# Block transforms of a state-space layer: float32 matrix products in place of three products of half-precision parts

## The chip, the cores and the metric

The kernel runs on one core of a Trainium2 chip. The metric is the device time of one execution in microseconds (us). A profiled execution beside it gives each engine's instructions: TensorE (PE, its weight loads PEld), VectorE (DVE), ScalarE (ACT), GpSimd (POOL) and the queues that issue transfers, above all SyncE's (SP).

## The reference

A sequence x of 2048 rows and 512 channels passes two layers. Each adds a long convolution of its normalised rows, and then a gated feed-forward product of the normalised result:

```
x = x + ssm(layernorm(x)); x = x + ffn(layernorm(x))     # twice, same weights
ssm(u): K[d, l] = Re(sum_n C[d, n] exp(dt A[d, n] l) dt B[d, n]);  y = causal_conv(u, K) + u * Dskip
ffn(x): (silu(x @ w_gate) * (x @ w_up)) @ w_down          # 512 -> 1376 -> 512
```

The reference makes the convolution by FFTs of length 4096. All is float32.

## The kernel before

**Blocks.** The sequence is cut into four blocks of 512 rows. The convolution works on block spectra: the block is normalised, transformed forward (`forward`, line 257), multiplied channel by channel with the filter's spectra, summed over the block and the earlier ones, and transformed back (`inverse`, line 770). Block b of a layer needs b + 1 products of spectra, so blocks 0 to 3 cost VectorE very different amounts. Eight (layer, block) pairs are worked in the order `SEQ` = (0,0), (0,1), (0,2), (1,0), (0,3), (1,1), (1,2), (1,3).

**Stages.** About the first 300 us make the filter's spectra and the split weights from the parameters; their order on the engines is written out by hand (`plan`, `at`). From then on the eight feed-forward blocks run, each as two halves of 256 rows (`ffn`, line 918). The loop at the end issues the convolution of pair i + 1 ahead of the feed-forward of pair i, and a scheduler that ranks instructions by given priorities sets the order on each engine when the program is built; the order is then fixed and each engine works its list from the front.

**A half of the feed-forward.** TensorE makes ten times 24 products of 128x256 half-precision tiles (lines 930, 931 and 933: the weights and the activations are each split in a high and a low half-precision part, three products for one), 48 small ones for the 96 columns that are left over (897 to 899), and 66 products 512 wide for the second matrix (945 to 947). VectorE multiplies gate and up (937), makes the low part (939) and adds the result to the block (950, twice per half). PSUM for these comes from one pool of two large buffers (`pbig`).

**The convolution.** One pass over a half of the channels (`ssm_half`, line 746) does four spectra. For each, line 810 multiplies two 128x1024 tiles and line 813 adds them up (first spectrum: 810 alone), 818 and 819 join the complex parts, 765 and 766 are butterflies; 831 to 843 prepare four tiles for `inverse`, and `result` (line 786) adds the result to the block. The first two pairs take their forward spectra by `direct` or `second`, and their inverse transform by float32 products.

**What the change touches.** From pair (0,2) on, both transforms use the way of the feed-forward. In `forward`, line 265 (ACT) and line 266 (through the helper `stt`, whose instructions carry line 230 on DVE) split the normalised tile n in two half-precision parts z; line 275 issues three products per pair of tiles; 276 to 278 scale and combine. In `inverse`, line 774 (ACT) and 775 (`stt`, line 230) split each tile v in parts yl, scaled by `sy`, and line 782 issues six products where the float32 branch issues two. The scale `sy` is made at run time: `sizes` (line 614) sums the magnitudes of the taps on ACT, once for each of eight chunks of channels, `direct_size` adds the skip term, and `product_scale` turns it into powers of two. The generator `inputs` (line 710) yields forward spectra, and `ssm_half` takes the next one from it at each of its four steps, so that one spectrum is ready ahead.

Of the kernel before, what the change touches and what calls it, by code (L numbers as in the profile page):

```python
# [22 lines left out]
P = 128  # L23
# [16 lines left out]
HALF = 2  # L40
INV = 2
# [4 lines left out]
def dft_constants():  # L46
# [21 lines left out]
    halves = []  # L68
    for e in (er * 256.0, ei * 8192.0):
        hi = e.astype(np.float16)  # L70
        halves.append(np.stack([hi, (e - hi).astype(np.float16)], 3))
    return [a.astype(np.float32) for a in (ef, ei, ek)] + [am] + halves
# [3 lines left out]
def kernel(ctx, tc, x, a_re, a_im, b_re, b_im, c_re, c_im, log_dt, d_skip,  # L76
                           w_gate, w_up, w_down, c_ef, c_ei, c_ek, c_am, c_eh, c_eih, out):
# [53 lines left out]
    wsum = sb.tile([P, NCH], F32, name="wsum")  # L131
    sy = sb.tile([P, 4], F32, name="sy")
    wmax = sb.tile([P, 2], BF16, name="wmax")
# [55 lines left out]
    dmax = sb.tile([1, 1], F32, name="dmax")  # L189

    def direct_size():

        da = tl([1, D], "da", "sg")
        A.activation(da, dsk, AF.Abs)
        V.tensor_reduce(dmax, da, axis=AX.X, op=OP.max)

# [60 lines left out]
    def forward(n, h, eh):  # L257


        if not fss:  # L260
            ft = tl([P, 3, 2, HD], "fbt", "bt")
            fss.extend([ft[:, i] for i in range(3)] + [tl([P, 2, HD], "fu", "u") for _ in range(3)])
            fs.extend(fss)
        hs = slice(h * HD, (h + 1) * HD)
        A.activation(z2[:, 0], n[:, :, hs], AF.Copy, scale=256.0)
        stt(z2[:, 1], n[:, :, hs], 256.0, z2[:, 0], OP.subtract)
        sums = []
        for pair in ((0, 2), (1, 3)):
            d_, s_ = fs.pop(0), fs.pop(0)
            pf = [psml([P, 2, HD], "pf") for _ in pair]  # L270
            with tc.high_priority(offset=BOOST):
                for r, p in zip(pair, pf):
                    for i in range(2):
                        for k, (le, lz) in enumerate(((0, 0), (0, 1), (1, 0))):
                            PE.matmul(p[:, i], lhsT=eh[:, r, i, le], rhs=z2[:, lz, r], start=k == 0, stop=k == 2)
                A.activation(d_, pf[0], AF.Copy, scale=2.0 ** -16)
            stt(s_, pf[1], 2.0 ** -16, d_, OP.add)
            stt(d_, pf[1], -2.0 ** -16, d_, OP.add)
# [333 lines left out]
    def sizes(ch, kt, junk):  # L612

        A.activation(junk, kt, AF.Abs, accum_out=wsum[:, ch:ch + 1])

    def product_scale():

        V.tensor_reduce(sy[:, 0:1], wsum, axis=AX.X, op=OP.max)  # L620
        V.tensor_tensor(sy[0:1, 0:1], sy[0:1, 0:1], dmax, OP.add)
# [680 lines left out]
```

## Time and profile before

| what | value |
|---|---|
| median of 3 runs | 1112.01 us (1109.95 to 1116.78) |
| the profiled execution | 1118.76 us, of which the span of its instructions is 1117.0 us |
| granted TensorE clock over the span | 0.982 |
| matrix products recorded | 9302 |
| bytes moved by transfers | 149.23 MB |

The profile lists for each engine the time in which it was busy. A matrix product's record is longer than the distance to the next one (they are pipelined), and DVE's records overlap a little in the same way, so the price of one in a full queue is the distance between two starts. In a row of groups stands the source line, the engine, the tile written and those read, the shape, the count, the busy time, the mean of one in ns, and the idle time of the engine just before them with what ended it. In a row of the time line stand the start, the length, the engine and line, and in brackets the idle time before it with its releaser. A row of stages gives for a stretch of the span each engine's busy time, the granted clock (1.00 is full speed) and the share of the transfer engines.

### The profile page before, as it was taken

To read this page: it belongs to the slowest core of one execution; us is meant where nothing else is said; L and a number is where in the kernel's file an instruction comes from. 1 tells how busy PE (TensorE), PEld (TensorE's weight loads), DVE (VectorE), ACT (ScalarE), POOL (GpSimd) and SP (SyncE) were. 2 spreads that over 40 slices of the span, in tenths; PEclk is the share of its full clock that TensorE was granted. 3 is DMA by queue.
4 is the path that set the end of the run, shared out by engine and by line. 5 is a ranking of instruction groups with operands and counts; after the bars stand their busy time and mean duration, and the time that the engine had idled before them with its cause. 6 is when DMAs were issued, how large, how long until landed. Compare 5 with 4: busy or idle time off the path is not lost.

```text
span 1117.0 us, 22795 instructions
## 1 busy us (share of the span) xinstructions
PE 1034.6 (93%) x9302; PEld 812.1 (73%) x9302; DVE 969.8 (87%) x1405; ACT 548.9 (49%) x1093; POOL 105.1 (9%) x163
## 2 busy tenths in 40 slices
PE   2989999998788999899999999989999999999998
PEld 1868888887676768686858677767768686786774
DVE  8999999999999998999999989999994899972221
ACT  6989999942483245464553154524315532143210
POOL 0112222220000010110000011100000000000000
PEclk9989999998999999999999999999999999999999
DMA  5367777767765455422453562354343244302000
GB/s 207 123 174 174 170 169 178 186 182 269 234 214 96 147 158 188 152 76 54 146 141 100 144 210 86 109 167 112 132 138 109 67 138 147 123 20 56 2 25 20
DMA packets 125003, 149.23 MB, mean 134 GB/s; under 512 B 50897, under 2 KB 75985, under 8 KB 124130
## 3 DMA queue, kind: packets, MB, share of 16 engines
q1 hardware_dynamic: 112994, 122.27, 36.1%
q0 software_dynamic: 11904, 25.50, 9.8%
q8 instruction: 73, 1.20, 0.5%
q14 instruction: 32, 0.26, 0.1%
HBM read 97.66 MB, written 33.82 MB: 118 GB/s over the span
## 4 chain that ended last, share of the span: by engine, by line
DVE 43%; PE 32%; issue 11%; DMA 7%; ACT 4%; POOL 2%; SPq 1%; DVEq 0%; POOLq 0%; ACTq 0%
PE pgu L930 5%; PE pgu L933 4%; PE pgu L931 4%; PE pw L542 4%; DVE t L810 4%; DVE yk L813 3%; DVE yk L810 3%; DMA mix<-nn 3%; DVE g L483 3%; PE py L945 3%; PE py L946 2%; PE py L947 2%; DMA n<-xdr 2%; DVE sg L937 2%; DVE g L497 2%
## 5 line engine op out<-in xcount | busy, mean ns | idle before, releaser
L930 PE MATMUL pgu<-mix,wsl 128*128 128x256 f16 x1280 | 300.4, 274 | 11.9 <-DVE sg L937 5.3
L931 PE MATMUL pgu<-mix,wsl 128*128 128x256 f16 x1280 | 300.2, 274 | 0.0
L933 PE MATMUL pgu<-mix,wsl 128*128 128x256 f16 x1280 | 196.2, 274 | 0.0
L945 PE MATMUL py<-wsl,hh 128*128 128x512 f16 (+1 forms) x352 | 136.0, 386 | 17.8 <-DVE xg L950 15.0
L931 PEld LDWEIGHTS <-wsl 128*128 128x128 f16 x1280 | 125.7, 98 | 31.1 <-issue 14.3
L930 PEld LDWEIGHTS <-wsl 128*128 128x128 f16 x1280 | 125.7, 98 | 18.5 <-issue 1.2
L947 PE MATMUL py<-wsl,hl 128*128 128x512 f16 (+1 forms) x352 | 135.7, 385 | 1.9 <-DVE hl L939 1.8
L933 PEld LDWEIGHTS <-wsl 128*128 128x128 f16 x1280 | 125.8, 98 | 15.5
L946 PE MATMUL py<-wsl,hh 128*128 128x512 f16 x320 | 123.8, 387 | 0.0
L936 ACT ACTIVATE sg<-pgu,sc 128x512 f32<-128x512 f32 x80 | 54.5, 681 | 137.0 <-PE pgu L933 136.9
L813 DVE TENSOR_TENSOR yk<-yk,t 128x1024 f32<-128x1024 f32 x96 | 116.7, 1215 | 0.4
L810 DVE TENSOR_TENSOR t<-uu,w 128x1024 f32<-128x1024 f32 x96 | 116.6, 1215 | 0.1
L937 DVE SCALAR_TENSOR_TENSOR sg<-pgu,sc,sg 128x512 f32<-128x512 f32 x80 | 59.5, 744 | 54.6 <-ACT sg L936 54.5
L938 ACT ACTIVATE hh<-sg 128x512 f16<-128x512 f32 x80 | 50.2, 627 | 86.9 <-DVE sg L937 86.9
L542 PE MATMUL pw<-kt,ek 128*128 128x256 f32 (+1 forms) x384 | 90.8, 373 | 0.0
L542 PEld LDWEIGHTS pw<-kt,ek 128*128 128x128 f32 x384 | 72.3, 193 | 8.5
L946 PEld LDWEIGHTS <-hh 128*128 128x128 f16 (+1 forms) x352 | 34.9, 99 | 56.8 <-issue 21.7
L507 PE MATMUL pk<-re,g 128*32 128x64 f32 x1024 | 65.1, 317 | 2.7 <-DMA g<-g 1.6
L939 DVE TENSOR_TENSOR hl<-sg,hh 128x512 f16<-128x512 f32 x80 | 54.7, 684 | 14.4 <-ACT hh L938 14.4
L947 PEld LDWEIGHTS <-hl 128*128 128x128 f16 (+1 forms) x352 | 34.9, 99 | 43.4 <-issue 3.0
L508 PE MATMUL pk<-im,g 128*32 128x64 f32 x1024 | 63.2, 301 | 0.0
L945 PEld LDWEIGHTS <-hh 128*128 128x128 f16 (+1 forms) x352 | 34.9, 99 | 35.6 <-issue 2.9
(265 smaller groups left out, 2007.1 us busy)
## 6 DMA issues: line engine op xcount, KB each, us to landing
uu<-udr SPq DMA_DIRECT2D x96, 256.0 KB, 3.0
w<-wdr SPq DMA_DIRECT2D x96, 256.0 KB, 2.7
g<-g POOLq DMA_DIRECT2D x6, 1024.0 KB, 9.1
udr<-fu POOLq DMA_DIRECT2D x22, 256.0 KB, 2.9
udr<-u SPq DMA_DIRECT2D x16, 256.0 KB, 3.4
n<-xdr SPq DMA_DIRECT2D x4, 1024.0 KB, 7.1
kdr<-ks SPq DMA_DIRECT2D x6, 512.0 KB, 3.1
kt<-kdr SPq DMA_DIRECT2D x24, 128.0 KB, 3.0
```

What stands on the lines that cost most here:

```text
L507: PE.matmul(o, lhsT=g[:, 0, :, d], rhs=re[:, 0:64, d], start=True, stop=False, tile_position=(0, 32 * grp))
L508: PE.matmul(o, lhsT=g[:, 1, :, d], rhs=im[:, 0:64, d], start=False, stop=True, tile_position=(0, 32 * grp))
L542: PE.matmul(pw[:, i], lhsT=e, rhs=kt[:, :, c + 4 * k0:4 * k1:4, :].rearrange("p g k d -> p k g d"), start=c == 0, stop=c == 3)
L810: V.tensor_tensor(t, uu.unsqueeze(2).to_broadcast([P, NQ, 2, 2, DC]), w.unsqueeze(3).to_broadcast([P, NQ, 2, 2, DC]), OP.mult)
L813: V.tensor_tensor(yk, yk, t, OP.add)
L930: PE.matmul(o, lhsT=wgu(wi, k, 0)[:, fs], rhs=nh[:, k], start=k == 0, stop=False)
L931: PE.matmul(o, lhsT=wgu(wi, k, 1)[:, fs], rhs=nh[:, k], start=False, stop=False)
L933: PE.matmul(o, lhsT=wgu(wi, k, 0)[:, fs], rhs=nlo[:, k], start=False, stop=k == 3)
L937: V.scalar_tensor_tensor(sg, pgu[:, 1], sc6[:, 4:5], sg, OP.mult, OP.mult)
L945: PE.matmul(py[:, r], lhsT=hh[:n, f, rc], rhs=wd(f, 0)[:n], start=f == 0, stop=False)
L946: PE.matmul(py[:, r], lhsT=hh[:n, f, rc], rhs=wd(f, 1)[:n], start=False, stop=False)
L947: PE.matmul(py[:, r], lhsT=hl[:n, f, rc], rhs=wd(f, 0)[:n], start=False, stop=f == FT - 1)
```

## The change

The half-precision parts of both block transforms go. `forward` multiplies n by float32 constants in one product per pair of tiles; `inverse` has only its float32 branch; the adds behind them lose their scale factors. `sizes`, `direct_size`, `product_scale` and the tiles z, yl, `sy` and `eih` go with them, and the two halved constant tables (512 KB each) give way to one float32 table `er` of 512 KB. Two buffers for forward spectra are added (`fz`, in the room of z), and from the third pair on `ssm_half` holds two spectra ahead instead of one.

```diff
-    def forward(n, h, eh):
+    def forward(n, h):
         if not fss:
-            ft = tl([P, 3, 2, HD], "fbt", "bt")
-            fss.extend([ft[:, i] for i in range(3)] + [tl([P, 2, HD], "fu", "u") for _ in range(3)])
+            ft, fz = tl([P, 3, 2, HD], "fbt", "bt"), tl([P, 2, 2, HD], "fz", "z")
+            fss.extend([ft[:, i] for i in range(3)] + [fz[:, i] for i in range(2)])
+            fss.extend(tl([P, 2, HD], "fu", "u") for _ in range(3))
             fs.extend(fss)
         hs = slice(h * HD, (h + 1) * HD)
-        A.activation(z2[:, 0], n[:, :, hs], AF.Copy, scale=256.0)
-        stt(z2[:, 1], n[:, :, hs], 256.0, z2[:, 0], OP.subtract)
...
                     for i in range(2):
-                        for k, (le, lz) in enumerate(((0, 0), (0, 1), (1, 0))):
-                            PE.matmul(p[:, i], lhsT=eh[:, r, i, le], rhs=z2[:, lz, r], start=k == 0, stop=k == 2)
-                A.activation(d_, pf[0], AF.Copy, scale=2.0 ** -16)
-            stt(s_, pf[1], 2.0 ** -16, d_, OP.add)
-            stt(d_, pf[1], -2.0 ** -16, d_, OP.add)
+                        PE.matmul(p[:, i], lhsT=er[0][:, r, i], rhs=n[:, r, hs], start=True, stop=True)
+                A.activation(d_, pf[0], AF.Copy)
+            V.tensor_tensor(s_, d_, pf[1], OP.add)
+            V.tensor_tensor(d_, d_, pf[1], OP.subtract)
...
-    def sizes(ch, kt, junk):
-        A.activation(junk, kt, AF.Abs, accum_out=wsum[:, ch:ch + 1])
...
         def inverse(pi, r, v):
-            if half:
-                yl = yl2[0][:, r % 2]
-                A.activation(yl[:, 0], v, AF.Copy, scale=sy[:, 0:1])
-                stt(yl[:, 1], v, sy[:, 0:1], yl[:, 0], OP.subtract)
             with tc.high_priority(offset=0 if first else BOOST):
-                if half:
-                    terms = [(eih[:, r, i, le], yl[:, ly, i]) for i in range(2) for le, ly in ((0, 0), (0, 1), (1, 0))]
-                else:
-                    terms = [(ei[:, r, i], v[:, i]) for i in range(2)]
-                for k, (e, o) in enumerate(terms):
-                    PE.matmul(pi[:, r % 2], lhsT=e, rhs=o, start=k == 0, stop=k == len(terms) - 1)
+                for i in range(2):
+                    PE.matmul(pi[:, r % 2], lhsT=ei[:, r, i], rhs=v[:, i], start=i == 0, stop=i == 1)
             done(v)
...
-            if half:
-                stt(o, pi, sy[:, 1:2], o, OP.add)
-            else:
-                V.tensor_tensor(o, o, pi, OP.add)
+            V.tensor_tensor(o, o, pi, OP.add)
...
+        depth = 1 if SEQ.index((layer, b)) < 2 else 2
...
-            nxt = next(spec, None)
-            if nxt:
+            while len(ahead) < depth and (nxt := next(spec, None)):
                 ahead.append(nxt)
```

Since the scheduler ranks anew, the lists of all engines change from about the first feed-forward products on. Two places on VectorE matter below.

The first is the inverse transform of pair (0,2), near the end of the first feed-forward block's second half. In the rows, line 831 to 843 prepare the tiles (`bb`, `mix`), `yl` is the low half-precision part, `yk` and `t` are the sums and products of spectra of the pair. Before:

```order
L831 TENSOR_TENSOR bb<-bb,mix 128x512
L950 SCALAR_TENSOR_TENSOR xg<-py,sc_92,xg 128x512
L813 TENSOR_TENSOR yk<-yk,t 128x1024
L834 TENSOR_TENSOR mix<-bb 128x256
L835 TENSOR_TENSOR mix<-bb 128x256
L839 TENSOR_TENSOR bb<-bb,mix 128x512
L230 SCALAR_TENSOR_TENSOR yl_4065<-bb,sy,yl_4065 128x512
L810 TENSOR_TENSOR t<-uu,w 128x1024
L842 TENSOR_TENSOR bb<-bb 128x256
L843 TENSOR_TENSOR bb<-bb 128x256
L230 SCALAR_TENSOR_TENSOR yl_4065<-mix,sy,yl_4065 128x512
```

Now, where the changed source's lines 773 to 785 are the former 831 to 843, 755 the former 813, 752 the former 810, 848 the former 906, 892 the former 950 and 734 the result's add:

```order
L773 TENSOR_TENSOR bb<-bb,mix 128x512
L881 TENSOR_TENSOR hl<-sg_3019,hh 128x512
L755 TENSOR_TENSOR yk<-yk,t 128x1024
L776 TENSOR_TENSOR mix<-bb 128x256
L777 TENSOR_TENSOR mix<-bb 128x256
L781 TENSOR_TENSOR bb<-bb,mix 128x512
L752 TENSOR_TENSOR t<-uu,w 128x1024
L784 TENSOR_TENSOR bb<-bb 128x256
L785 TENSOR_TENSOR bb<-bb 128x256
L848 SCALAR_TENSOR_TENSOR sg_3019<-pgu,sc_92,sg_3019 128x192
L892 SCALAR_TENSOR_TENSOR xg<-py,sc_92,xg 128x512
```

The low parts are gone. Before, the row of line 950 is the half's second result, and most of the tiles stand behind it; now the row of line 892 is the half's first result, and all of them stand ahead of it: the convolution stands earlier against the feed-forward.

The second place is the end of the first feed-forward half, VectorE's list up to its second result (line 950, now 892). `fu`, `fbt` and `fz` are forward spectra of pair (0,2). Before:

```order
L818 TENSOR_TENSOR bb<-yk 128x256
L819 TENSOR_TENSOR bb<-yk 128x256
L810 TENSOR_TENSOR t<-uu,w 128x1024
L290 TENSOR_TENSOR fbt<-fbt 128x4x64 x2
L290 TENSOR_TENSOR fu<-fbt 128x4x64 x2
L765 TENSOR_TENSOR bb<-mix,bb 128x512
L810 TENSOR_TENSOR yk<-fu,w0r 128x1024
L950 SCALAR_TENSOR_TENSOR xg<-py,sc_92,xg 128x512
```

Now:

```order
L760 TENSOR_TENSOR bb<-yk 128x256
L761 TENSOR_TENSOR bb<-yk 128x256
L752 TENSOR_TENSOR t<-uu,w 128x1024
L734 TENSOR_TENSOR xg<-xg,pi 128x2x256
L752 TENSOR_TENSOR yk<-fu,w0r 128x1024
L734 TENSOR_TENSOR xg<-xg,pi 128x2x256
L755 TENSOR_TENSOR yk<-yk,t 128x1024
L258 TENSOR_TENSOR fz<-fbt,pf 128x512
L752 TENSOR_TENSOR t<-uu,w 128x1024
L892 SCALAR_TENSOR_TENSOR xg<-py,sc_92,xg 128x512
```

The first half's list holds 41 instructions of lines 810 and 813 where it held 34: more of the products of pair (0,2) stands ahead of the first half's end. Counted the same way, between one half's second result and the next one's, the sixteen halves hold 34, 20, 20, 8, 23, 19, 21, 17, 19, 20, 8, 22, 23, 2, 0, 0 of them before and 41, 21, 16, 20, 25, 23, 24, 19, 12, 0, 13, 25, 17, 0, 0, 0 now.

On TensorE, between the ends of the halves' last products of line 947, the lists hold of the block transforms: in the first half 24 half-precision products of `forward` and 24 float32 products of `inverse` before, 12 and 32 float32 products now; in the next seven halves 360 half-precision products and 8 float32 ones before, 140 float32 ones now; in the last eight 192 half-precision ones before and 40 float32 ones now.

56 lines of the change are left out of this document (7 added, 49 removed).

## The prediction

> **What bounds the kernel now.** I read the busy shares first, then the stages, then TensorE's waits, then the places where feed-forward halves end.
>
> ```profile
> PE 1034.6 (93%) x9302; PEld 812.1 (73%) x9302; DVE 969.8 (87%) x1405; ACT 548.9 (49%) x1093; POOL 105.1 (9%) x163
> ```
>
> ```profile
> 0.00:298.00 298.00, 260.17 (x2981) 226.22 (x2982) 285.14 (x397) 223.09 (x462) 55.54 (x94) 0.98 0.69 188
> 298.00:372.50 74.50, 64.69 (x499) 49.66 (x499) 72.50 (x111) 41.01 (x87) 4.57 (x8) 0.93 0.62 164
> 372.50:840.50 468.00, 442.94 (x3632) 334.92 (x3630) 447.80 (x670) 198.24 (x385) 37.50 (x51) 0.99 0.43 132
> 840.50:1117.00 276.50, 266.80 (x2195) 201.31 (x2193) 164.40 (x232) 86.58 (x160) 7.53 (x10) 1.00 0.24 69
> ```
>
> The stages are columns of stretch, length, PE, PEld, DVE, ACT, POOL, clock, transfer share, GB/s. Up to 298 us the filter is made, and VectorE is busy for 285 of 298 us. From 298 to 372.5 runs the first feed-forward half, VectorE 72.5 of 74.5 us. From 372.5 to 840.5 run nine halves, with VectorE and TensorE both near 95%. Only from 840.5 on does VectorE have room (164 of 276.5 us) while TensorE is full. So the question is which of two nearly full engines the change helps.
>
> ```profile
> PE py L945 <- DVE xg L950: 15.0, 7, 3.8
> PE pgu L930 <- DVE sg L937: 5.3, 6, 2.5
> PE pgu L897 <- DVE sg L937: 4.8, 3, 3.2
> PE pi L782 <- ACT yl L774: 1.6, 2, 1.0
> ```
>
> From 300 us on, what TensorE waits for (total us, times, longest) is nearly always VectorE, which comes late to a feed-forward result that stands behind long products of spectra in its list. The parts that the change removes appear with 1.6 us alone. Some waits cost twice:
>
> ```profile
> 588.43 0.27 PE L930 MATMUL pgu<-mix,wsl 128*128 128x256 f16 x1 [1.95 <-DVE xf L950]
> 732.91 0.59 PE L945 MATMUL py<-wsl,hh 128*128 128x512 f16 x1 [3.78 <-DVE xg L950]
> ```
>
> ```profile
> 590.00:600.00 10.00, 10.00 (x81) 8.41 (x80) 9.97 (x14) 1.95 (x3) 0.00 (x0) 0.86 0.53 167
> 730.00:740.00 10.00, 7.09 (x26) 2.92 (x26) 9.97 (x15) 0.36 (x1) 0.80 (x2) 0.83 0.31 105
> ```
>
> Behind a gap of 1.95 us the granted clock is 0.86 over ten us, behind one of 3.78 us 0.83. By the stage rows the clock took 0.07 x 74.5 + 0.01 x 468 = about 10 us from 298 to 840.5.
>
> ```profile
> 371.81 0.75 DVE L950 SCALAR_TENSOR_TENSOR xg<-py,sc,xg 128x512 f32<-128x512 f32 x1
> 744.25 0.74 DVE L950 SCALAR_TENSOR_TENSOR xg<-py,sc,xg 128x512 f32<-128x512 f32 x1
> 1070.99 0.75 DVE L950 SCALAR_TENSOR_TENSOR xg<-py,sc,xg 128x512 f32<-128x512 f32 x1 [5.41 <-PE py L947]
> 1112.45 0.75 DVE L950 SCALAR_TENSOR_TENSOR xg<-py,sc,xg 128x512 f32<-128x512 f32 x1 [7.38 <-PE py L947]
> ```
>
> These are second results of halves: of the first, the eighth, the fifteenth and the last. The last half, with no convolution beside it, took 41.5 us; halves two to eight took 372.4 us, or 53.2 each; the last eight took 368.2 us, or 46.0 each.
>
> **The change part by part.** *TensorE.*
>
> ```profile
> 229.34 0.59 PE L542 MATMUL pw<-kt,ef 128*128 128x256 f32 x2
> 229.77 1.46 PE L542 MATMUL pw<-kt,ek 128*128 128x256 f32 x6
> 231.06 0.59 PE L542 MATMUL pw<-kt,ef 128*128 128x256 f32 x2
> ```
>
> ```profile
> 1050.13 0.60 PE L933 MATMUL pgu<-mix,wsl 128*128 128x256 f16 x4
> 1051.44 0.60 PE L933 MATMUL pgu<-mix,wsl 128*128 128x256 f16 x4
> ```
>
> ```profile
> L782 PE MATMUL pi<-yl,mix 128*128 128x256 f16 x288 | 43.0, 272 | 1.9 <-ACT yl L774 1.6 <-DVE yl L230 0.3
> L275 PE MATMUL pf<-z,eh 128*128 128x256 f16 x288 | 37.6, 273 | 1.2 <-ACT z L265 1.2
> L782 PE MATMUL pi<-bb,mix 128*128 128x256 f32 x48 | 13.5, 407 | 3.1 <-DVE bb L831 3.0
> L782 PE MATMUL pi<-mix 128*128 128x256 f32 x16 | 5.1, 447 | 0.0
> ```
>
> In a full queue eight float32 records start in 231.06 - 229.34 = 1.72 us, 0.215 us each. The two first pairs issue 32 float32 products in `inverse`, and the trace has 48 + 16 = 64 records, so one product is two records and costs 0.43 us. Twelve half-precision products start in 1.31 us (1050.13 to 1051.44; the eight between are lines 930 and 931), 0.109 us each, so the three that one product replaces cost 0.327 us. The 288 + 288 half-precision products are 192 triples, and TensorE gains 192 x (0.43 - 0.327) = **20 us** of work.
>
> *VectorE.*
>
> ```profile
> 752.32 1.21 DVE L813 TENSOR_TENSOR yk<-yk,t 128x1024 f32<-128x1024 f32 x1
> 753.45 0.68 DVE L939 TENSOR_TENSOR hl<-sg,hh 128x512 f16<-128x512 f32 x1
> 754.05 0.74 DVE L230 SCALAR_TENSOR_TENSOR yl<-mix,sy,yl 128x512 f16<-128x512 f32 x1
> 754.71 0.41 DVE L818 TENSOR_TENSOR mix<-yk 128x256 f32<-128x256 f32 x1
> ```
>
> ```profile
> L230 DVE SCALAR_TENSOR_TENSOR yl<-bb,sy,yl 128x512 f16<-128x512 f32 x32 | 23.7, 742 | 3.6 <-ACT yl L774 3.6
> L230 DVE SCALAR_TENSOR_TENSOR yl<-mix,sy,yl 128x512 f16<-128x512 f32 x16 | 11.9, 742 | 0.4 <-ACT yl L774 0.4
> L230 DVE SCALAR_TENSOR_TENSOR z<-n,z 128x1024 f16<-128x1024 f32 x12 | 14.6, 1215 | 3.2 <-ACT z L265 3.2
> ```
>
> From start to start a 128x1024 pass takes 1.13 us, a yl 0.66 and a plain pass over 512 columns 0.60. So 12 z and 48 yl give back 12 x 1.13 + 48 x 0.66 = 45 us, the 24 results 24 x 0.06 = 1.4, the scale some 1: **about 48 us**. The 7.2 us in which VectorE waited for ACT ahead of them go too.
>
> *ScalarE.*
>
> ```profile
> L774 ACT ACTIVATE yl<-bb,sy 128x512 f16<-128x512 f32 x32 | 22.9, 719 | 39.4 <-DVE bb L831 28.0 <-PE pi L782 7.9 <-DVE bb L835 3.3
> L614 ACT ACTIVATE ks<-kt 128x1024 f32<-128x1024 f32 x8 | 9.3, 1164 | 0.0
> ```
>
> ACT loses the taps' sums (9.3 us) and, by the same durations, 48 yl and 12 z, some 56 us in all. It is busy 49% of the span; up to 298 us its eight sums stand beside a VectorE that is full and does not read them, so I cost them at nothing, at most 9 us if each was on the path. The two constant tables saved are 0.5 MB of 149 and are loaded beside other work: nothing.
>
> **The sum, by halves.** What the engines' lists hold between the ends of halves is counted, with 42.4 us of products for a feed-forward half (240 x 0.109, 66 of twice the width at 0.216, 48 small; the last half's 41.5 us confirms it) and the prices above. Before, halves two to eight hold 339 us for TensorE and 353 for VectorE and took 372; the last eight hold 358 and 250 and took 368. In each half the larger load is what must pass: 353 and 360 us summed over halves, so 19.5 and 8 us are lost to coupling and to the clock.
>
> Now halves two to eight hold 357 us for TensorE and 359 for VectorE, and the larger of each half adds up to 362; the last eight hold 355 and 185, the larger 355. The saving in VectorE's list thus lies almost wholly in the last eight halves, where it was idle anyway, because the new lists pull the products of spectra forward. The first half's list grows by about 10 us on VectorE (seven products or sums at 1.13 and some small passes) and 6 us on TensorE.
>
> - First half: VectorE is full there, so its 10 us nearly count: between 0 (they go into the 2 us of idle time and into waits that I don't see) and 10. I take +8.
> - Halves two to eight: 362 plus coupling. At most the former 19.5, at least 5, since less waits on ACT but both engines are now equally full. I take 15: 377, or +5.
> - Last eight halves: 355 plus 7 where 8 was lost: 362, or -6.
>
> The sum is +8 + 5 - 6 = +7 us. The profiled execution's span would go from 1117.0 to 1124, its time from 1118.76 to 1125.8. The median shown is 6.75 us below that execution, so I predict **1119 us**.
>
> *A rule weighed.* The Trainium skill, page "TensorE: Matmul & The Clock Gate", section "HAM oscillation — how this bites in real kernels", asks for no TensorE gaps above about 3.4 us. This trace has the lower clock behind a gap of 1.95 us already, so the measurement decides. By the page's bound short gaps like that one would cost nothing, and fewer of them would not bring back any clock; by the rows each saved is worth over a microsecond.
>
> **Rivals.**
>
> *TensorE sets the end, and its gaps stay: 1132 us.* The whole 20 us is paid and the 48 us of VectorE are worth nothing. For it: TensorE is the busiest engine, the new halves two to eight load both engines equally, so every late result still stops it, and a longer wait lowers the clock. Against: VectorE's overhang over TensorE of 353 - 339 = 14 us in these halves, which stopped TensorE, falls to 2. It decides if halves two to eight take more than 383 us with the first half's end after 380.
>
> *The gaps close: 1096 us.* With VectorE no longer late, the 10 us of clock come back, halves two to eight take 367, the last eight 358, and the first half ends 5 us later: 371.8 + 5 + 367 + 358 + 4.5 behind the last result = 1106 in the span, -11; with no loss at all it is 371.8 + 362 + 355 + 4.5 = 1093, -24. I put it midway, at -16. For it: TensorE's waits all end on VectorE, and the chain tile, ACT part, VectorE part, product loses two links. Against: the lists do not give the freed time to the full halves. The Trainium skill, page "Perfetto Trace Analysis", section "Identifying the Most-Contended Engine", would judge TensorE by weight loads, 73% here, below VectorE's 87%, and so favour this rival.
>
> *The second spectrum ahead moves the stall.* Forward spectra need the block that a feed-forward half has just stored; asked for earlier, the load waits at the front of SP's list, and behind it the loads of w and uu for lines 810 wait too.
>
> ```profile
> n<-xdr SPq DMA_DIRECT2D x4, 1024.0 KB, 7.1
> ```
>
> Four such loads take 7.1 us to land. If each stopped VectorE for that long, it would be 28 us and 1140; as VectorE has other work in most of these places, I count it as a part of the slower cases.
>
> **How the numbers follow.** A measurement of this kernel tells about 1% from no change, so same is 1101 to 1123. My forecast's own range, with coupling of 5 to 19.5 us and the first half at 0 to +10, is 1101 to 1125 (0 - 5 - 6 = -11 to 10 + 9 - 6 = +13). I give it 0.5, TensorE's rival 0.25, the moved stall 0.05, the closed gaps 0.2. Most of the forecast lies within 1%, with its upper end beyond: faster 0.22, same 0.44, slower 0.34. The range for 8 in 10 reaches to the closed gaps and past the slower rival: 1097 to 1136.
>
> **What would show it.** Right: no ACT or VectorE rows for z and yl; float32 rows of both transforms at 0.215 us from start to start; the second result of the first half near 381 us, of the eighth near 758; VectorE idle for most of the last eight halves, and TensorE full there. Wrong: if the eighth half ends before 745 us the gaps have closed, and if TensorE's waits for line 892 grow beyond the 15 us of line 950, the slower rival holds.

## The result, and the profile after

The changed kernel takes 1126.86 us (median of 4 runs, 1124.76 to 1128.5) and the kernel before 1112.12 us in the same call: a ratio of 1.0126, 95% interval 1.0090 to 1.0162. It is slower by 1.3%. The forecast was 1119 us within 1097 to 1136, with the sign left nearly open (0.34 for slower); the narrower range of my own forecast, 1101 to 1125, ends 2 us short of it.

The profiled execution after took 1128.5 us, with a span of 1126.7 us. That is 1.6 us above its median, where the profiled execution before stood 6.75 us above its own. So the spans of the two profiles differ by 9.7 us and the medians by 14.7; the 5 us between these are a property of which execution was profiled. In which stages of before they lie cannot be read, so a difference of a few us between a stage of before and the same stage of another run is no firmer than that.

The busy shares of after:

```profile
PE 1052.3 (93%) x9109; PEld 828.1 (74%) x9109; DVE 924.2 (82%) x1335; ACT 497.7 (44%) x1016; POOL 102.4 (9%) x163
```

Against before TensorE has 17.7 us more, VectorE 45.6 less and ACT 51.2 less. There are no rows for z, yl or their split any more. The groups of float32 products (line, engine, tiles, shape, count, then busy time and mean) are these:

```profile
L256 PE MATMUL pf<-n,er 128*128 128x256 f32 x192 | 47.3, 380 | 0.7 <-ACT n L236 0.7
L728 PE MATMUL pi<-bb,mix 128*128 128x256 f32 x176 | 47.1, 397 | 3.8 <-DVE bb L773 3.8
L728 PE MATMUL pi<-mix 128*128 128x256 f32 x80 | 21.3, 386 | 0.0
```

The forward transform has 192 records for 96 products and the inverse 256 where it had 64. A run of twelve of them in the time line gives their price:

```profile
463.91 2.76 PE L256 MATMUL pf<-n,er 128*128 128x256 f32 x12
```

From the first start to the last end are 2.76 us; less the 0.38 us of one record (the mean of the group), eleven distances remain, (2.76 - 0.38) / 11 = 0.216 us each. Two such records make one product, 0.43 us.

The second results of the first half, the eighth and the last:

```profile
385.48 0.74 DVE L892 SCALAR_TENSOR_TENSOR xg<-py,sc,xg 128x512 f32<-128x512 f32 x1
762.82 0.74 DVE L892 SCALAR_TENSOR_TENSOR xg<-py,sc,xg 128x512 f32<-128x512 f32 x1
1122.06 0.75 DVE L892 SCALAR_TENSOR_TENSOR xg<-py,sc,xg 128x512 f32<-128x512 f32 x1 [7.38 <-PE py L889]
```

The first half ends 13.7 us later than before (385.5 against 371.8). Halves two to eight take 377.3 us, 4.9 more. The last eight take 359.2 us, 9.0 less. The sum is +9.7, that of the spans. Cut at these ends, the stages of before and then of after (stretch, length, PE, PEld, DVE, ACT, POOL, clock, transfer share, GB/s):

```profile
0.00:371.81 371.81, 324.17 (x3473) 275.26 (x3474) 356.95 (x504) 264.10 (x548) 60.10 (x102) 0.97 0.67 183
371.81:744.25 372.44, 350.78 (x2880) 266.07 (x2879) 355.17 (x536) 164.60 (x324) 32.98 (x43) 0.99 0.43 130
744.25:1112.45 368.20, 359.64 (x2954) 270.78 (x2951) 256.97 (x366) 120.22 (x221) 12.05 (x19) 1.00 0.30 89
```

```profile
0.00:385.48 385.48, 334.94 (x3495) 285.51 (x3496) 367.57 (x518) 257.69 (x539) 63.06 (x103) 0.95 0.65 180
385.48:762.82 377.34, 362.53 (x2765) 275.48 (x2763) 362.19 (x545) 142.33 (x292) 32.80 (x48) 1.00 0.46 141
762.82:1122.06 359.24, 354.88 (x2854) 267.14 (x2851) 193.74 (x276) 97.64 (x185) 6.53 (x13) 1.00 0.25 71
```

VectorE's column is the one to read. It lost 63 us in the last eight halves, where it was idle anyway. In halves two to eight it gained 7.0, and ahead of the first half's end 10.6. The whole saving of 45.6 us lies where it buys little. Up to the end of the eighth half VectorE has 17.6 us more to do than before (729.8 against 712.1), and that end comes 18.6 us later.

What TensorE waits for from 300 us on (total, times, longest):

```profile
PE pgu L872 <- DVE sg L879: 15.5, 7, 4.5
...
PE py L887 <- DVE xg L892: 3.7, 3, 1.6
```

The former first wait, for the result in xg, has shrunk from 15.0 to 3.7 us. The wait for sg, the product of gate and up (line 879, formerly 937), has grown, and three of its seven stand in the first half:

```profile
326.00 0.37 PE L872 MATMUL pgu<-mix,wsl 128*128 128x256 f16 x1 [3.37 <-DVE sg L879]
336.80 0.27 PE L872 MATMUL pgu<-mix,wsl 128*128 128x256 f16 x1 [2.67 <-DVE sg L879]
355.61 0.37 PE L872 MATMUL pgu<-mix,wsl 128*128 128x256 f16 x1 [4.45 <-DVE sg L879]
```

Together they are 10.5 us. When sg comes, in before and then in after:

```profile
317.85 0.74 DVE L937 SCALAR_TENSOR_TENSOR sg<-pgu,sc,sg 128x512 f32<-128x512 f32 x1
324.23 0.74 DVE L937 SCALAR_TENSOR_TENSOR sg<-pgu,sc,sg 128x512 f32<-128x512 f32 x1
332.82 0.74 DVE L937 SCALAR_TENSOR_TENSOR sg<-pgu,sc,sg 128x512 f32<-128x512 f32 x1
337.69 0.74 DVE L937 SCALAR_TENSOR_TENSOR sg<-pgu,sc,sg 128x512 f32<-128x512 f32 x1
```

```profile
325.20 0.75 DVE L879 SCALAR_TENSOR_TENSOR sg<-pgu,sc,sg 128x512 f32<-128x512 f32 x1 [1.51 <-ACT sg L878]
336.01 0.73 DVE L879 SCALAR_TENSOR_TENSOR sg<-pgu,sc,sg 128x512 f32<-128x512 f32 x1
339.68 0.74 DVE L879 SCALAR_TENSOR_TENSOR sg<-pgu,sc,sg 128x512 f32<-128x512 f32 x1
354.81 0.74 DVE L879 SCALAR_TENSOR_TENSOR sg<-pgu,sc,sg 128x512 f32<-128x512 f32 x1
```

The first is 7.4 us later, and before the fourth are 15.1 us without one. VectorE is never idle in those 15 us. Its list has convolution there, some of it of pair (0,2) (lines 258 and 259 are that pair's forward transform):

```profile
342.21 1.21 DVE L752 TENSOR_TENSOR t<-uu,w 128x1024 f32<-128x1024 f32 x1
...
346.49 1.21 DVE L752 TENSOR_TENSOR yk<-u,w0r 128x1024 f32<-128x1024 f32 x1
347.74 1.23 DVE L755 TENSOR_TENSOR yk<-yk,t 128x1024 f32<-128x1024 f32 x1
348.88 0.68 DVE L258 TENSOR_TENSOR fbt<-fbt,pf 128x512 f32<-128x512 f32 x1
...
353.08 1.22 DVE L752 TENSOR_TENSOR yk<-u,w0r 128x1024 f32<-128x1024 f32 x1
354.22 0.68 DVE L258 TENSOR_TENSOR fz<-fbt,pf 128x512 f32<-128x512 f32 x1
```

What else changed in the order is to be seen on ACT, where the hand-written stage ends. First before, then after:

```profile
313.31 1.05 ACT L614 ACTIVATE ks<-kt 128x1024 f32<-128x1024 f32 x1
...
314.47 1.28 ACT L936 ACT_TABLE_LOAD   x1
315.76 0.69 ACT L936 ACTIVATE sg<-pgu,sc 128x512 f32<-128x512 f32 x1
```

```profile
318.97 0.63 ACT L204 ACTIVATE junk<-n 128x512 bf16<-128x512 f32 x1 [3.11 <-DMA n<-in_A_u_dram]
...
323.18 1.28 ACT L878 ACT_TABLE_LOAD   x1
324.48 0.69 ACT L878 ACTIVATE sg<-pgu,sc 128x512 f32<-128x512 f32 x1
```

Before, the sum over the last chunk's taps was ACT's last instruction of that stage, and the first sg followed it at once. Now the row statistics of pair (0,2) stand there, which wait 3.11 us for a transfer, and what follows on VectorE stands in another order. Whether the missing sum brought this order about, and whether the order, the pulled work or the price of the products makes the kernel slower, the experiments are to tell.

### The profile page after: what moved, and what is told of

Same layout as the page of the kernel before. It is cut to its first block, busy times and chain, and to the rows that moved or that the text cites. A ratio compares the mean times of both kernels' runs of the same rounds, so it can differ in the third digit from the quotient of the medians.

```text
span 1126.7 us, 22234 instructions
## 1 busy us (share of the span) xinstructions
PE 1052.3 (93%) x9109; PEld 828.1 (74%) x9109; DVE 924.2 (82%) x1335; ACT 497.7 (44%) x1016; POOL 102.4 (9%) x163
## 4 chain that ended last, share of the span: by engine, by line
PE 47%; DVE 15%; DMA 5%; ACT 3%; issue 3%; SPq 2%; POOL 0%; DVEq 0%; ACTq 0%; POOLq 0%
PE pgu L872 9%; PE pgu L873 8%; PE pgu L875 8%; PE py L887 5%; PE py L888 5%; PE py L889 5%; PE pi L728 3%; DVE t L752 2%; DVE yk L755 2%; PE pf L256 2%; DMA n<-xdr 2%; DMA mix<-nn 2%; DVE yk L752 2%; SPq L853 1%; ACT junk L204 1%
## 5 line engine op out<-in xcount | busy, mean ns | idle before, releaser
L887 PE MATMUL py<-wsl,hh 128*128 128x512 f16 (+1 forms) x352 | 133.5, 379 | 8.2 <-DVE xf L892 3.8
L889 PE MATMUL py<-wsl,hl 128*128 128x512 f16 (+1 forms) x352 | 133.4, 379 | 2.1 <-DVE hl L881 2.1
L888 PE MATMUL py<-wsl,hh 128*128 128x512 f16 x320 | 121.3, 379 | 0.0
L523 PE MATMUL pw<-kt,ek 128*128 128x256 f32 (+1 forms) x384 | 93.8, 382 | 0.0
L523 PEld LDWEIGHTS pw<-kt,ek 128*128 128x128 f32 x384 | 75.2, 200 | 8.8
L888 PEld LDWEIGHTS <-hh 128*128 128x128 f16 (+1 forms) x352 | 34.5, 98 | 44.6 <-issue 8.2
```

Source lines behind the costliest of these rows:

```text
L523: PE.matmul(pw[:, i], lhsT=e, rhs=kt[:, :, c + 4 * k0:4 * k1:4, :].rearrange("p g k d -> p k g d"), start=c == 0, stop=c == 3)
L887: PE.matmul(py[:, r], lhsT=hh[:n, f, rc], rhs=wd(f, 0)[:n], start=f == 0, stop=False)
L888: PE.matmul(py[:, r], lhsT=hh[:n, f, rc], rhs=wd(f, 1)[:n], start=False, stop=False)
L889: PE.matmul(py[:, r], lhsT=hl[:n, f, rc], rhs=wd(f, 0)[:n], start=False, stop=f == FT - 1)
```

## The experiments

Each is compared with the kernel before on the same chip. "First half", "two to eight" and "last eight" are read as above from the second results.

### One spectrum ahead

```diff
-        depth = 1 if SEQ.index((layer, b)) < 2 else 2
+        depth = 1
```

> The changed kernel with one spectrum ahead at every step, as before; the float32 products stay. My theory (the time is the sum of the first feed-forward half, stretched by what the lists pull into it, and of the larger engine load of each later half): its VectorE list holds the same 41 products and sums of spectra in the first half and the same loads later, so the first half still ends near 385 us and the time is that of the changed kernel, within 4 us. Rival (the second spectrum ahead moves a stall, or pulls the work into the first half): without it the first half ends near 372 us and some 10 us or more come back.

1129.7 us, ratio 1.0126 [1.0087, 1.0165]: the same as the full change. The first half ends at 384.04, two to eight take 379.1, the last eight 360.8. Making spectra two steps ahead has no effect that can be measured.

### Only the inverse in float32, only the forward in float32

Both start from the kernel before. In the first, the inverse takes its float32 branch throughout (`INV = 8`):

> The kernel before with only the inverse transforms by float32 products; forward transforms stay in three half-precision products, and the sums of the taps still run though nothing uses them. My theory: the first half's list is as before (34 products and sums, end near 372 us); halves two to eight 362 us of the larger load plus 15, the last eight 357 plus 7: about 1 to 3 us above before. Rival (TensorE's work alone sets the time): 96 x 0.105 = 10 us above before.

1121.35 us, ratio 1.0074 [1.0047, 1.0101]. First half 372.05, two to eight 378.6, last eight 365.5. The first half stays as it was, and the loss is in halves two to eight, +6.2 us. In all it is about 8 us where I had put 1 to 3: the total is nearer to the rival's 10. But VectorE too has 8.9 us more to do in these halves (364.0 against 355.2), so the run does not tell TensorE's work from VectorE's.

In the second, `forward` is the changed kernel's and `inverse` is that of before:

```diff
-        A.activation(z2[:, 0], n[:, :, hs], AF.Copy, scale=256.0)
-        stt(z2[:, 1], n[:, :, hs], 256.0, z2[:, 0], OP.subtract)
...
-                        for k, (le, lz) in enumerate(((0, 0), (0, 1), (1, 0))):
-                            PE.matmul(p[:, i], lhsT=eh[:, r, i, le], rhs=z2[:, lz, r], start=k == 0, stop=k == 2)
+                        PE.matmul(p[:, i], lhsT=eh[:, r, i], rhs=n[:, r, hs], start=True, stop=True)
...
```

> The kernel before with only the forward transforms by float32 products; inverse transforms stay in half-precision parts. My theory: the first half's list grows by 2.5 us on VectorE and 3.5 us on TensorE, so its end is near 375 us; halves two to eight 364 plus 15, the last eight 361 plus 7: about 8 us above before. Rival (TensorE's work alone): 10 us above before, which these totals do not tell apart; the stages do, as the rival has the first half unchanged and the ten us spread over the eight blocks.

1130.87 us, ratio 1.0145 [1.0112, 1.0177]. First half 376.62, two to eight 375.1, last eight 371.8. The first half ends where I had put it, but the run costs some 16 us instead of 8, by itself as much as the whole change, and fits neither theory. VectorE has 726.0 us to do up to the end of the eighth half, 13.9 more than before and nearly as much as in the full change (729.8). The two parts give 0.74% and 1.45% and together 1.26%: they do not add. Each builds another order, so the effects of edits cannot be added up to better than several us here.

### One product for three: less work for TensorE

From the changed kernel, the float32 products of the pairs from (0,2) on become single products of the upper halves of the same words (the lower 16 bits are left out). VectorE's work stays the same in sum, but not in its place.

```diff
+    def upper_half(t):
+        return t.bitcast(BF16)[..., 1::2]
...
-                        PE.matmul(p[:, i], lhsT=er[0][:, r, i], rhs=n[:, r, hs], start=True, stop=True)
+                        PE.matmul(p[:, i], lhsT=upper_half(er[0])[:, r, i], rhs=upper_half(n)[:, r, hs], start=True, stop=True)
...
```

> The changed kernel, but from pair (0,2) on each float32 product of a block transform is one product of the operands' upper 16 bits (bfloat16), so the lower bits of these transforms are left out; VectorE's and ScalarE's work is as in the changed kernel. This takes 192 x (0.43 - 0.109) = 62 us from TensorE alone. My theory: halves two to eight hold 317 us of the larger load instead of 362, the last eight 343 instead of 355, the first half is nearly as late as in the changed kernel: 55 to 60 us less than the changed kernel. Rival (VectorE sets the stretch up to 840 us, TensorE's price is hidden): only the last eight halves gain, some 12 us.

```profile
PE 992.5 (92%) x8917; PEld 776.4 (72%) x8917; DVE 922.6 (86%) x1335; ACT 495.6 (46%) x1016; POOL 101.1 (9%) x163
```

1079.19 us, ratio 0.9680 [0.9642, 0.9718]. TensorE is busy 59.8 us less than in the changed kernel, and the median is 47.7 us lower (I had put it at 55 to 60): 0.8 us for each us that TensorE lost. Nearly all of it comes in halves two to eight (335.4 against 377.3). The stage rows of halves two to eight and of the last eight show that TensorE was not relieved alone:

```profile
382.56:717.99 335.43, 315.75 (x2584) 235.64 (x2584) 317.13 (x482) 134.64 (x281) 29.35 (x43) 0.99 0.46 140
717.99:1073.01 355.02, 344.00 (x2808) 256.35 (x2806) 238.32 (x338) 103.58 (x199) 9.29 (x18) 1.00 0.31 90
```

In halves two to eight TensorE is busy 46.8 us less than in the changed kernel (362.53), and VectorE 45.1 us less (362.19), because the new order holds 123 products and sums there instead of 148; VectorE's 44.6 us come back in the last eight halves. **So the 0.8 is not the price of TensorE's work alone: the relief of either engine would explain it.** And the first half still ends at 382.56, 10.8 us later than before, so the price of the float32 products is hardly what makes it late.

### No low parts: less work for VectorE

From the kernel before, VectorE's passes that make the low parts are left out, and the products read the high part twice. TensorE's work is unchanged.

```diff
-        stt(z2[:, 1], n[:, :, hs], 256.0, z2[:, 0], OP.subtract)
...
-                stt(yl[:, 1], v, sy[:, 0:1], yl[:, 0], OP.subtract)
...
```

> The kernel before with its three half-precision products per tile, but without VectorE's low parts z and yl (the product takes the high part in their place, so the low parts of the block transforms are left out): 45 us of VectorE's work and the waits on it go, TensorE's work stays. My theory (in the lists the freed time goes to the last halves, where VectorE was idle anyway): larger loads of 359 + 350 + 354 where before has 356 + 353 + 360, so about 6 us less than before. Rival (VectorE sets the stretch up to 840 us): 30 us or more less than before.

```profile
PE 1029.6 (93%) x9302; PEld 811.2 (73%) x9302; DVE 925.9 (84%) x1345; ACT 548.4 (50%) x1093; POOL 100.8 (9%) x163
```

1110.72 us, ratio 0.9980 [0.9964, 0.9996]. VectorE has 43.9 us less and the time falls by some 2 us (I had put it at 6, the rival at 30 or more), about 0.05 us for each us that VectorE lost (0.01 to 0.09 by the interval: 0.0004 to 0.0036 of 1113 us over 43.9). The stage rows of halves two to eight and of the last eight show where the relief lies:

```profile
374.86:742.83 367.97, 348.00 (x2861) 264.13 (x2860) 351.39 (x533) 173.04 (x342) 32.01 (x45) 0.99 0.46 140
742.83:1101.09 358.26, 353.81 (x2921) 267.07 (x2919) 214.32 (x305) 110.83 (x203) 8.80 (x16) 1.00 0.27 81
```

In the last eight halves VectorE has 42.7 us less than before (256.97), in halves two to eight only 3.8 less. **So this is the price of relief in the last eight halves, where VectorE had room.** The change's relief lies in the same place, so it should be worth as little, although VectorE was busy 87% of the span. What VectorE's work costs ahead of that, the run does not show.

### The hold: are the pulled products the first half's loss?

One small VectorE instruction takes the yk buffer that products of pair (0,2) need, and gives it back after the first half. It keeps those products out of the first half: 33 products and sums of 128x1024 stand in its list instead of 41.

```diff
+            if layer == 0 and b == 0 and s == 0:
+                hold = tl([P, 1], "hold", "y1")
+                V.tensor_scalar(hold, xt[:, rows - 1, 0:1], 1.0, None, OP.mult)
```

> The changed kernel, with one pass of one element added behind the first half's second result; it fills the buffer of the sums yk, so no product of pair (0,2) can stand in the first half any more (33 products and sums there instead of 41). My theory (the products pulled forward stretch the first half, where both engines and the clock suffer): the first half ends near 375 us instead of 385, halves two to eight take the larger loads of 357 plus 15, the last eight 359 plus 6: 6 to 9 us less than the changed kernel. Rival (work pulled forward is work saved later; VectorE's total counts): the later halves lose what the first gains, and the time is that of the changed kernel within 3 us.

1122.4 us, ratio 1.0081 [1.0062, 1.0101]. The first half still ends at 384.43; two to eight take 367.0, the last eight 364.5. I had put that end near 375, so my reason for the first half's length, the pulled products, failed in this form. In all the run is some 5 us faster than the changed kernel, between my 6 to 9 and the rival's 3: the gain lies in halves two to eight, where VectorE has 7.0 us less (355.2 against 362.2). The stage up to the first half's end shows what happened there:

```profile
0.00:384.43 384.43, 335.22 (x3500) 285.10 (x3501) 360.27 (x511) 260.05 (x543) 62.72 (x103) 0.96 0.64 178
```

VectorE has 7.3 us less work there than in the changed kernel (360.27 against 367.57), but is idle for 24.2 us (384.43 - 360.27) instead of 17.9. What it waits for in the first half, and did not in the changed kernel, stands in its own waits:

```profile
DVE xg L734 <- PE pi L728: 4.5, 2, 3.2
```

The products of spectra had filled waiting time. Without them VectorE waits for TensorE, and TensorE still waits for the sg that stand late in the list (9.3 us in this half, 10.5 in the changed kernel).

### A third of the float32 transforms, with the hold

Here the pairs (0,2) and (1,0) use float32 products, and those from (0,3) on half-precision ones (`HALF = INV = 4` in the kernel before, whose `forward` gets the changed one's branch): two of the six pairs that the change touches. One spectrum ahead, with the hold.

> Float32 products for the block transforms of pairs (0,2) and (1,0) alone, the half-precision parts from (0,3) on, one spectrum ahead, and the hold of the first half as in the run before last. Theory by larger loads: 356 + 359 + 353 against 356 + 353 + 360 before, so the time of before within 3 us. By TensorE's work alone: 64 x 0.105 = 7 us above before.

1114.87 us, ratio 1.0013 [0.9998, 1.0028]. First half 375.02, two to eight 374.5, last eight 359.8. It is no faster than the kernel before, and within the 3 us of my theory; by TensorE's work alone I had put it 7 us above.

### The kernel before with the hold

The same three lines in the kernel before:

> The kernel before with the same hold behind the first half's second result and nothing else. Its first half loses one product of pair (0,2). Theory by larger loads: 355 + 350 + 361 against 356 + 353 + 360, so 2 to 3 us less than before; the rival (the hold is one more wait and nothing was in the way) has it 0 to 3 us slower.

1107.7 us, ratio 0.9952 [0.9935, 0.9969]. First half 374.15, two to eight 363.7, last eight 367.3. **It is the fastest of all versions that keep the computation.** But the gain is not in the first half, which holds one product less and ends 2.3 us later than before. It is in halves two to eight, 8.7 us shorter, where VectorE has 5.9 us less (349.25 against 355.17) and the last eight halves have some 6 more: the hold moved work there through the order it led to.

### The last sum put back

If the order at the end of the hand-written stage is the cause, one ACT instruction should bring it back. To the changed kernel the sum over the last chunk's taps is added at the same place in the program; nothing reads it.

```diff
+    wsum = sb.tile([P, 1], F32, name="wsum")
...
+        A.activation(ks, kts[1], AF.Abs, accum_out=wsum)
```

> The changed kernel with one instruction put back: ScalarE's sum over the last chunk's taps at the end of the hand-written order (its result is not used). By the list this makes the VectorE work between the first half's feed-forward results even again (7.3, 8.2, 3.8, 6.5, 7.1, 5.5 us instead of 10.6, 3.7, 15.0, 1.3, 7.7, 9.6), with 36 products and sums in that half instead of 41; the block's row statistics still stand ahead of the first sg on ScalarE. Theory (the scheduler's order of that stretch cost the first half its time): first half ends near 375 us instead of 385.5, halves two to eight take about 374, the last eight 364, span 1118, 8 or 9 us below the changed kernel, ratio to before about 1.005. Rival (the float32 products' own work, or the statistics ahead of the first sg, made the first half longer): it ends at 383 to 386 again, and the ratio stays at 1.012.

1119.81 us, ratio 1.0065 [1.0042, 1.0088]. First half 379.35 (I had put it at 375), two to eight 373.3, last eight 361.4, span 1119.1.

```profile
0.00:379.35 379.35, 329.41 (x3510) 280.11 (x3511) 358.64 (x507) 252.60 (x531) 65.50 (x102) 0.96 0.65 181
```

**An instruction of 1 us that does nothing useful takes about half of the change's loss away.** VectorE has 358.64 us of work ahead of that end where the changed kernel has 367.57; its idle time there rises from 17.9 to 20.7 us. So the gain is work that the new order has moved behind the first half: VectorE has 2.6 us less in halves two to eight as well, and 10.1 more in the last eight. The old order does not come back. The statistics still stand ahead of the first sg on ACT, and of the first four sg on VectorE the first comes later still than in the changed kernel (325.20) and the fourth earlier (354.81):

```profile
327.74 0.75 DVE L880 SCALAR_TENSOR_TENSOR sg<-pgu,sc,sg 128x512 f32<-128x512 f32 x1 [2.76 <-ACT sg L879]
...
347.07 0.74 DVE L880 SCALAR_TENSOR_TENSOR sg<-pgu,sc,sg 128x512 f32<-128x512 f32 x1
```

So it is not the late start that made the difference.

### The last sum and the hold

> The changed kernel with that one sum put back and also the hold that keeps the next block's last products out of the first half (33 products and sums there). The loads by the lists are 355.5 us of VectorE in the first half, 360.5 for halves two to eight, 358.7 for the last eight: 1075, as with the hold alone, 9 below the changed kernel, 6 above the kernel before. Theory (even order and fewer pulled products both count): first half ends at 373 to 375, halves two to eight take 367 to 372, the last eight 364, span 1109 to 1116, ratio 0.997 to 1.003. Rival (both mend the same thing): span 1118 to 1121 as with the hold alone or the sum alone, ratio 1.005 to 1.008.

1117.86 us, ratio 1.0038 [1.0025, 1.0052]. First half 374.30, two to eight 371.4, last eight 364.6, span 1115.4: each as expected, and the ratio 0.0008 above the range I gave.

```profile
0.00:374.30 374.30, 324.86 (x3500) 275.62 (x3501) 355.39 (x505) 252.87 (x531) 63.99 (x102) 0.96 0.66 183
```

This differs from the hold alone by the one sum. The same 33 products and sums stand in the first half, and it ends 10.1 us earlier: 4.9 less work and 5.3 less idle time. Halves two to eight take 4.4 more, of which 3.7 is work that the other list had ahead of the boundary. The later halves hold the same numbers of products and sums in both. So the order inside the first half alone is worth 0.4% (1.0081 to 1.0038). And with all the float32 products of the change in it, this kernel is only 0.38% slower than the one before.

### The converse: the kernel before without its last sum

```diff
-        V.tensor_reduce(sy[:, 0:1], wsum, axis=AX.X, op=OP.max)
+        V.tensor_reduce(sy[:, 0:1], wsum[:, :NCH - 1], axis=AX.X, op=OP.max)
...
-        sizes(c, kts[1], ks)
```

> The converse on the kernel before: all its half-precision products and splits stay, and only ScalarE's sum over the last chunk's taps is left out (the scale is made from the other seven chunks' sums, which is the part of the computation changed). 1.2 us of ScalarE work less, but the VectorE work between the first half's feed-forward results becomes uneven: 9.4, 1.8, 10.8, 3.1, 10.0, 6.0 us instead of 6.4, 8.1, 4.9, 5.0, 5.8, 13.1. Theory (order): first half ends at 379 to 384 instead of 371.8, halves two to eight take 368 to 370 (their load falls by 3.6), the last eight 368, span 1121 to 1126, ratio 1.003 to 1.008. Rival (float32 products made the first half longer): the first half ends near 372 as before, span 1112 to 1116, ratio 0.996 to 1.000.

1116.66 us, ratio 1.0026 [1.0008, 1.0045]. First half 380.22, two to eight 367.3, last eight 365.2, span 1117.3.

```profile
0.00:380.22 380.22, 332.63 (x3523) 285.04 (x3524) 360.65 (x510) 263.82 (x547) 62.43 (x102) 0.96 0.64 180
```

The first half ends 8.4 us later, with all half-precision products in place: 3.7 us more work by VectorE and 4.7 more idle time. So float32 is not what it takes to make the first half long. But most of the delay came back later, 5.1 us in halves two to eight and 3.0 in the last eight, so the span is hardly longer and the time rises by 0.3%, a little below what I expected (span 1121 to 1126, ratio from 1.003). Of those 8.1 us, 3.8 is work that already lies behind (VectorE's load in halves two to eight falls that much). Some 2.5 us more need not have come back at all: the spans of the two profiles differ by 0.3 us and the medians by 2.9, as the profiled execution of before was a long one. The rest is not settled.

## Why the prediction was right, and where it was not

**Prices.** Each was right to a few us. A float32 product takes 0.43 us; TensorE gained 17.7 us of busy time where 20 was forecast, VectorE lost 45.6 for 48 and ACT 51.2 for 56. For TensorE the agreement is partly luck: the same products are busy 1044.6 us in the run with the last sum and the hold, only 10.0 more than before, so busy time depends on the order too.

**Where the freed time lies.** Right, and it carries the prediction: VectorE's saving fell into the last eight halves (-63 us there), and halves two to eight got 7 us more. The run without low parts shows the same from the other side: its relief lies there too and buys some 2 us.

What the forecast did not name is how closely the time follows VectorE's work up to the end of the eighth half. In all thirteen kernels VectorE is idle for only 26 to 36 us ahead of that end, so the end moves with its work: 712.1 us of work and the end at 744.2 before, 729.8 and 762.8 now, 683.5 and 718.0 with one product for three, 714.3 and 745.7 with the last sum and the hold. This is a pattern over kernels that each have another order; no run moves VectorE's work alone, and TensorE's busy time over the whole span goes with the measured times about as well. But the last of the four has all the float32 products of the change and nearly the early VectorE work of before, and costs 0.38% instead of 1.26%. So 0.9 of the 1.26% goes with the order, at the same products. With the hold in the kernel before too (0.9952, and 705.3 us of VectorE's work up to that end), the difference is again 0.9%, or some 10 us; what it would be at the best order of each is not known.

**Halves two to eight.** +5 was forecast, +4.9 was measured, and coupling came to 377.3 - 362 = 15 us, as taken. That it came so close is partly luck: 15 was chosen between 5 and 19.5 without a row that gives it, and the profiled execution before was a long one. TensorE's waits for xg fell from 15.0 to 3.7 us instead of growing, so the sign that was to speak for the slower rival did not come.

**Last eight halves.** -6 was forecast, -9.0 measured; the loss beside the load is 359.2 - 355 = 4 us where I kept 7. The loads are a little too large: the ninth half now takes 41.3 us (762.82 to 804.15), where 42.4 was counted for its feed-forward products alone.

**The first half.** This is the term that was mis-sized: +8 between 0 and 10 was forecast, +13.7 was measured. Its reason was half of the truth. VectorE's 10 us more are there (10.6), and I let part of them vanish into idle time. Instead the idle time rose too, by 3.0 us. VectorE's waits from 297 us on stand ahead of its first sg: 1.5 us for weights from ACT, 1.6 us for the row statistics and 1.5 us for ACT's part of sg. From 326 us to the half's end it is busy nearly without a break (59.2 of 59.5 us), so in this profile the late sg hold up TensorE but not the end of the half. What they cost TensorE shows in its gaps and in its clock:

```profile
320.00:330.00 10.00, 6.63 (x44) 5.04 (x42) 6.78 (x12) 9.97 (x25) 0.70 (x1) 0.74 0.82 254
330.00:340.00 10.00, 7.33 (x59) 6.16 (x58) 10.00 (x15) 7.87 (x14) 3.32 (x1) 0.92 0.55 179
350.00:360.00 10.00, 5.55 (x54) 4.31 (x51) 10.00 (x17) 1.42 (x3) 0.88 (x2) 0.83 0.20 59
```

The ten us that hold the three gaps (3.37, 2.67 and 4.45 us) show 0.74, 0.92 and 0.83. Cut finer, the second of them reads otherwise:

```profile
326.00:328.00 2.00, 2.00 (x10) 1.45 (x10) 1.87 (x3) 2.00 (x5) 0.00 (x0) 0.50 1.00 280
330.00:332.00 2.00, 2.00 (x13) 1.52 (x12) 2.00 (x3) 2.00 (x4) 0.00 (x0) 0.60 0.00 0
334.00:336.00 2.00, 0.12 (x2) 0.00 (x0) 2.00 (x4) 0.07 (x1) 2.00 (x1) 1.00 0.31 61
336.00:338.00 2.00, 1.21 (x12) 1.07 (x12) 2.00 (x5) 1.82 (x3) 0.95 (x1) 1.00 0.61 193
```

The 0.92 is the rest of the slow stretch that began in the gap of 3.37 us; around the gap of 2.67 us (334.1 to 336.8) the clock is 1.00. The Trainium skill, page "TensorE: Matmul & The Clock Gate", section "HAM oscillation — how this bites in real kernels", puts the harmful gap at about 3.4 us. These three gaps agree with it, but before the change the lower clock already stood behind a gap of 1.95 us, so the length of a gap alone does not tell.

**ACT at nothing.** This step failed, and a part of the first half's delay comes from it (6.1 of 13.7 us, by the run that puts the sum back). I wrote that the eight sums stand up to 298 us beside a VectorE that does not read them. The eighth stands at 313.31, at the seam between the hand-written order and the scheduled one. Taking it away cost nothing in ACT's time and, by the same run, about half of the whole loss (1.0126 to 1.0065) through the order that came out without it. The converse run agrees for the first half (+8.4 us) and less for the whole (0.3%). I had counted what the new lists hold and not asked which single removal had made them new.

**The median.** I took the span's +7 and kept the 6.75 us by which the profiled execution before stood above its median. After, that was 1.6, so 5.1 of the 7.9 us between 1119 and 1126.9 are due to this and 2.7 to the stages.

**The rivals.** *TensorE sets the end, 1132 us*: that VectorE's relief is worth nearly nothing held, as far as it lies in the last eight halves; that TensorE's 20 us are paid whole is shown by no run, and the run with the last sum and the hold has the same products for 4 us. Of its two signs one came (the first half's end after 380) and one did not: two to eight took 377.3, below its 383. *The gaps close, 1096 us*: TensorE's idle time in halves two to sixteen did fall, from 30.2 to 19.2 us by the stage rows (740.6 - 710.4 and 736.6 - 717.4), but 7.0 us more of work stand against it there and the first half's loss beside it. The Trainium skill's page "Perfetto Trace Analysis", section "Identifying the Most-Contended Engine", would have named VectorE. Up to the end of the eighth half the rows of before agree with it (VectorE 712.1 of 744.2 us, TensorE's products 675.0); the run without low parts cannot test it, since its relief lies behind that end. *The second spectrum ahead*: no effect.

**What the agreement is worth.** The range of 1097 to 1136 was made to hold both rivals, so a time inside it says little for the mechanism. What speaks for it is the signs of the stages: up in the first half and in halves two to eight, down in the last eight.

**What stays open.** How much of the loss is TensorE's added work and how much VectorE's early work was not separated: that would take a run that changes one of them with the order held. Why the scheduler lays VectorE's work as it does in each kernel, the forward transform alone in float32 above all, was not taken apart.

## What to carry to other kernels

Before pricing a trade between two nearly full engines by runs that relieve each of them, read in which stage the relief falls: here 44 us of VectorE's work bought 2 us, since they lay where VectorE had room, and a run meant to relieve TensorE alone relieved VectorE too, because the order was made anew. Where a scheduler ranks instructions, an edit also reorders what it does not touch; look at the seam where the order changes, count each engine's work ahead of the point where it has room again, and try the removed instruction by itself before blaming the arithmetic. And compare medians with medians: a profiled execution may stand several us above its own.

## What was not expected of the hardware

TensorE's clock was lower after gaps of 3.37 and 4.45 us, down to 0.50 in a stretch of two us, but stayed at 1.00 around a gap of 2.67 us, while before the change it fell behind one of 1.95 us. An average over ten us can put a slow stretch beside the wrong gap. Beyond that the chip did what the rows of before had shown; the surprise was in the order.
